# Attention and two MLPs on one core: a new planned order, input rebuilding on GpSimd, one reciprocal, late normalisation and ScalarE's Silu

## The chip, the cores and the metric

The kernel runs on one core of a Trainium2 chip. A core has five engines, each with a queue of its own that runs in the order in which the program was emitted: TensorE (PE, matmuls), VectorE (DVE), ScalarE (ACT), GpSimd (POOL) and SyncE (SP, which issues the DMAs). They meet through semaphores. The metric is device microseconds of one launch. Most executions of this kernel agree within 0.3%.

## The reference

Attention over pairwise averaged queries gives `x`, and two MLPs follow, one with a leaky rectifier, one with `h * sigmoid(h)`.

```python
# q, k, v: [2, 8, 1152, 64] float32
q_pool = q.reshape(B, H, S // 2, 2, D).mean(axis=3)          # 576 queries
scores = np.matmul(q_pool, k.transpose(0, 1, 3, 2)) / np.sqrt(D)
scores = scores - np.max(scores, axis=-1, keepdims=True)
attn = np.exp(scores)
attn = attn / (np.sum(attn, axis=-1, keepdims=True) + 1e-09)
o = np.matmul(attn, v)
x = o.transpose(0, 2, 1, 3).reshape(1152, 512)
# w_in [512, 2048], w_out [2048, 512], float64
h = x @ moe_w_in;  x = np.maximum(0.01 * h, h) @ moe_w_out
h = x @ moe2_w_in; out = (h * (1.0 / (1.0 + np.exp(-h)))) @ moe2_w_out
```

## The kernel before

**Precision.** A float32 operand is held as a high part and a low part, and a product is the sum of three matmuls (high by high, high by low, low by high). The high part is a ScalarE copy, the low part a subtraction, on GpSimd for most tiles. The weights come as float64 and are turned into float32 by bit operations: one ScalarE step (L180), four VectorE steps on an accumulator bank or a buffer (L184, L188, L192, L199), for the layer-in weights also a copy (L205) and four sums (L219), and then the split into high (L227, ScalarE) and low (L231, GpSimd).

**Attention.** `attention()` works on eight pairs of heads. Each pair has score maxima (L571), scores (L693), exponentials (L699, ScalarE), their running sums (L737, VectorE or GpSimd), the product with the values (L751), and the normalisation. `finish()` normalises the first seven pairs (L871, L874, L877: product, high part, low part). The last pair is `end()`: sums over the partitions (L837), a copy (L843), two reciprocals of 128 x 288 (L851), two products (L852), high parts (L853) and low parts (L854). The normalised values stand in `xh` and `xl`.

**MLPs.** `mlps()` works on the 1152 tokens in two groups: group 0 is 512 tokens (two halves of 256), group 1 is 640 (two halves of 320). The 2048 hidden units of a layer are four blocks. The first block of the first layer is done in the plain way (`layer_in_plain`, matmul L1283): 144 matmuls. The seven others multiply by seven products of half-size operands instead of eight (`cell`, matmul L1329), which takes sums of the inputs ahead of it and sums of the products behind it. The sums of the inputs are `transform()`: four subtractions (L1173) from the input at full precision, high parts (L1187, ScalarE) and low parts (L1193: GpSimd, but two of group 1 in the second layer on VectorE). For the first layer the full-precision input is first put together again from `xh` and `xl` by `rebuild()` (L1207, eight VectorE instructions), into `acc1`. The sums of the products are L1351 on VectorE, behind a ScalarE copy (L1365). `rectify()` makes the hidden tile `g` from a cell's result: in the first layer two ScalarE passes (L1240 the high part, L1245 the full value), in the second a sigmoid (L1255), a product on GpSimd (L1259) and a copy (L1263); then the low part (L1235, GpSimd). `layer_out_t` is the first MLP's second matmul (L1398); its result is evacuated to `acc1` (L1415 by ScalarE for the first block, L1417 by VectorE), which for the first block waits until the transform has read the rebuilt input, since both use `acc1`. `layer_out` is the second MLP's second matmul (L1464).

**Order.** Both parts are planned by a list scheduler (`Plan`): every task has an engine, a weight, a due time and the tasks that it follows; of those ready, the one due first is emitted next on its engine. So the numbers in `PARAMS` set the order of the instructions in each queue, and nothing is reordered on the chip. The MLPs run through seventeen phases: in each, two layer-in units of one block and group with the layer-out of the block and group before. Accumulators are taken in pairs of banks (`duo`), and the product sums give them back.

In what follows, `late`, `a` and `acc` are full-precision buffers, `th`/`tl` and `xh`/`xl` the high and low parts of transformed and plain inputs, `w` and `more` layer-in weights, `wout` layer-out weights, `wt` the weight in conversion, `psum` an accumulator.

## Time and profile before

| | |
|---|---|
| median of three runs | 620.33 us (619.4 to 622.56) |
| the profiled execution | 619.83 us, of which its span is 618.0 us |
| TensorE, VectorE | 591.2 us (96%), 510.3 us (83%) |
| ScalarE, GpSimd | 336.9 us (55%), 391.6 us (63%) |
| mean granted TensorE clock | 0.981 of full |

The span goes from the first to the last instruction of the core. The shares are of the whole span. The granted clock has two levels, 1.2 and 2.4 GHz; a value between them is a mean over a stretch. The attention ends, for TensorE, at 207.93 us; the first layer's steady part is from 277.02 to 376.35 us and the second layer's from 448.99 us on.

### The profile page before, as it was taken

The numbers are of one execution on the slowest core, as the hardware profiler recorded it, in microseconds if no ns is written. First come the engines' busy times: TensorE is split into PE (matmuls) and PEld (weight loads), VectorE is DVE, ScalarE is ACT, GpSimd is POOL, SyncE is SP. The second block draws the span as 40 slices with busy tenths as digits, with TensorE's granted clock in tenths as the row PEclk, the third lists the DMA queues.
The fourth block names the chain that finished last, engine by engine and source line by source line (L and its number), as shares of the span: only waits on it lengthen the run. The fifth ranks groups of instructions, "written<-read, shape, count | busy, mean of one in ns | idle before, by whom it ended". The sixth has DMA issues, their size and how long they took to land.

```text
span 618.0 us, 11491 instructions
## 1 busy us (share of the span) xinstructions
PE 591.2 (96%) x4412; PEld 506.3 (82%) x4412; DVE 510.3 (83%) x808; ACT 336.9 (55%) x573; POOL 391.6 (63%) x268
## 2 busy tenths in 40 slices
PE   7989999999999987999999999897999999999997
PEld 5758668677678676999999998886988998998986
DVE  5899779798898899758988987999887888898433
ACT  4747558567458454665545544565476644554310
POOL 7966657648450158585465464689898759759721
PEclk9799999999999988899999999999899999999999
DMA  8032433443311122232332333222132332232012
GB/s 273 35 101 55 137 98 93 149 139 94 100 33 58 53 69 69 87 118 69 102 103 74 98 101 102 66 73 68 49 94 100 100 103 90 82 103 69 0 69 85
DMA packets 33119, 55.07 MB, mean 89 GB/s; under 512 B 13196, under 2 KB 14632, under 8 KB 33064
## 3 DMA queue, kind: packets, MB, share of 16 engines
q1 hardware_dynamic: 32920, 54.14, 28.3%
q8 instruction: 34, 0.56, 0.4%
q10 hardware_dynamic: 144, 0.20, 0.1%
q14 instruction: 21, 0.17, 0.1%
HBM read 49.81 MB, written 2.42 MB: 85 GB/s over the span
## 4 chain that ended last, share of the span: by engine, by line
PE 76%; DVE 12%; ACT 5%; issue 4%; POOL 2%; DMA 1%; SPq 0%; DVEq 0%; POOLq 0%; ACTq 0%
PE psum L1329 23%; PE psum L1464 15%; PE psum L1398 14%; PE psum L693 12%; PE psum L751 7%; PE psum L564 3%; DVE acc L1173 3%; DVE late L737 2%; ACT e L699 1%; DVE mx L571 1%; DVE acc L1207 1%; PE psum L596 1%; DVE late L1351 1%; DMA qnat<-in_q_dram 1%; PE psum L789 1%
## 5 line engine op out<-in xcount | busy, mean ns | idle before, releaser
L1398 PE MATMUL psum<-g,wout 128*128 128x320 f32 (+1 forms) x576 | 106.0, 342 | 4.3 <-ACT acc L1415 3.4
L1398 PEld LDWEIGHTS psum<-g,wout 128*128 128x128 f32 x576 | 93.8, 191 | 13.3 <-ACT acc L1415 3.8
L1464 PE MATMUL psum<-wout,g 128*128 128x512 f32 (+1 forms) x444 | 100.7, 384 | 0.3 <-DVE g L1235 0.2
L699 ACT ACTIVATE e<-psum 128x512 f32<-128x512 f32 (+1 forms) x144 | 88.7, 663 | 17.4 <-PE psum L693 15.1
L571 DVE TENSOR_REDUCE mx<-psum 128x2 f32<-128x768 f32 x96 | 87.9, 949 | 10.0 <-PE psum L564 9.0
L1464 PEld LDWEIGHTS psum<-wout,g 128*128 128x128 f32 x444 | 81.1, 188 | 16.7 <-DVE g L1235 0.7
L751 PE MATMUL psum<-e,vnat 128*64 128x320 f32 (+1 forms) x576 | 72.5, 408 | 0.1
L1351 DVE TENSOR_TENSOR late<-psum,late 128x256 f32<-128x256 f32 (+3 forms) x84 | 54.5, 653 | 21.4 <-PE psum L1329 18.9
L231 POOL TENSOR_TENSOR w<-wt,w 128x896 fp32r<-128x896 f32 (+1 forms) x18 | 35.6, 1982 | 52.1 <-ACT w L227 45.7
L1235 POOL TENSOR_TENSOR g<-a,g 128x512 fp32r<-128x512 f32 (+1 forms) x34 | 48.2, 1427 | 29.4 <-ACT a L1245 26.6
L737 DVE TENSOR_TENSOR late<-late,e 128x512 f32<-128x512 f32 (+1 forms) x77 | 63.7, 862 | 0.9
L751 PEld LDWEIGHTS psum<-e,vnat 128*64 128x64 f32 x576 | 40.3, 137 | 28.3 <-ACT e L699 1.4
L737 POOL TENSOR_TENSOR late<-late,e 128x512 f32<-128x512 f32 (+1 forms) x35 | 49.9, 1425 | 21.1 <-DVE late L737 13.8
L231 POOL TENSOR_TENSOR wout<-wt,wout 128x512 fp32r<-128x512 f32 x32 | 43.5, 1374 | 22.5 <-ACT wout L227 20.8
L1329 PE MATMUL psum<-xh,w 128*128 128x256 f32 (+1 forms) x224 | 50.8, 300 | 7.3 <-DVE late L1351 7.2
L693 PE MATMUL psum<-qh,kh 64*128 64x320 f32 (+1 forms) x288 | 49.6, 341 | 1.3 <-DVE mx L571 0.5
L1329 PE MATMUL psum<-xh,more 128*128 128x256 f32 (+1 forms) x224 | 49.7, 294 | 0.6 <-DVE late L1351 0.6
L184 DVE TENSOR_SCALAR psum<-psum 128x512 f32<-128x512 f32 x60 | 41.4, 691 | 10.3 <-ACT psum L180 10.1
L231 POOL TENSOR_TENSOR more<-wt,more 128x896 fp32r<-128x896 f32 x14 | 30.2, 2162 | 23.9 <-ACT more L227 20.6
L1329 PEld LDWEIGHTS psum<-xh,w 128*128 128x128 f32 x224 | 38.3, 191 | 8.3 <-DVE late L1351 7.7
L1235 POOL TENSOR_TENSOR g<-late,g 128x512 fp32r<-128x512 f32 (+1 forms) x28 | 41.2, 1488 | 4.3 <-ACT late L1245 3.2
L693 PE MATMUL psum<-row,onesr 64*128 64x320 f32 (+1 forms) x288 | 43.1, 295 | 0.0
(123 smaller groups left out, 1422.8 us busy)
## 6 DMA issues: line engine op xcount, KB each, us to landing
wraw<-in_moe_w_in_dram SPq DMA_DIRECT2D x32, 512.0 KB, 4.0
wraw<-in_moe_w_out_dram SPq DMA_DIRECT2D x32, 512.0 KB, 3.1
vnat<-in_v_dram SPq DMA_DIRECT2D x8, 576.0 KB, 4.7
knat<-in_k_dram SPq DMA_DIRECT2D x7, 576.0 KB, 5.6
qnat<-in_q_dram SPq DMA_DIRECT2D x7, 576.0 KB, 7.4
out_dram<-acc SPq DMA_DIRECT2D x8, 256.0 KB, 2.0
xl<-late SPq DMA_DIRECT2D x7, 288.0 KB, 4.5
xh<-d SPq DMA_DIRECT2D x14, 144.0 KB, 3.9
```

Of the source, the lines that this page charges most:

```text
L184: nc.vector.tensor_scalar(out=tf, in0=tf, scalar1=2.0, scalar2=W_TOP, op0=ALU.max, op1=ALU.min)
L231: self.nc.gpsimd.tensor_tensor(out=lo, in0=tf, in1=hi, op=ALU.subtract)
L571: nc.vector.tensor_reduce(out=mx[p][:, u, c], in_=ps[:, :, 0:KC], op=ALU.max, axis=AX.X)
L693: nc.tensor.matmul(out=ps[:, j, 0:n], lhsT=lhsT[own[j], :], rhs=rhs[own[j], cs], start=m == 0, stop=m == len(terms) - 1)
L699: nc.scalar.activation(out=e_t[h, t], in_=ps[:, :, 0:n], func=ACTF.Exp, scale=scale)
L737: e.tensor_tensor(out=a, in0=e_t[h, 0] if t == 1 else a, in1=e_t[h, t], op=ALU.add)
L751: nc.tensor.matmul(out=vps[h][0][own[j], 0, 0:CW[c]], lhsT=vnat[p][:, j, t, :], rhs=e_t[h, t][:, j, :], start=(t == 0), stop=(t == NKT - 1),)
L1235: (nc.vector if fast else nc.gpsimd).tensor_tensor(out=gl, in0=a(), in1=gh, op=ALU.subtract)
L1329: nc.tensor.matmul(out=box[key][:, bank, 0:n], lhsT=w[:, i, :], rhs=y, start=(kk == 0 and q == 0), stop=(kk == 1 and q == 2),)
L1351: nc.vector.tensor_tensor(out=to, in0=p, in1=y, op=ALU.add)
L1398: nc.tensor.matmul(out=box[x][:, c, 0:n], lhsT=wt[:, ms], rhs=y[:, c * n:(c + 1) * n], start=(f == 0 and y is gh and wt is oh), stop=(f == ...
L1464: nc.tensor.matmul(out=box[x][:, c, 0:n], lhsT=y[:, ts], rhs=wt[:, cs], start=(f == 0 and y is gh and wt is oh), stop=(f == FB - 1 and y i ...
```

## The change

All of the plan's numbers are new, and several new ones are added, among them a table of the order of layer-in and layer-out in each phase (`orders`). The rest is named in the diff's pieces below.

```diff
 def end():
-            for c in range(2):
-                for j in range(2):
-                    nc.tensor.matmul(
-                        out=box["end"][own[j], c, 0:C], lhsT=ones, rhs=acc[p][:, j, c * C:(c + 1) * C], start=True, stop=True
-                    )
+            for i, j, c, rows in quarters:
+                nc.tensor.matmul(
+                    out=box["end"][rows, 0, 0:C], lhsT=ones[:, 0:32], rhs=acc[p][:, j, c * C:(c + 1) * C], start=True, stop=True
+                )
...
+        def factors():
+            nc.vector.reciprocal(out=rec[p], in_=rec[p])
+
+        def spread():
+            for i, j, c, rows in quarters:
+                nc.tensor.matmul(out=box["end"][own[j], c, 0:C], lhsT=pick[rows, :], rhs=rec[p][rows, :], start=True, stop=True)
...
 def finish(p, factors, values, due):
+        if p >= NP - 1 - P["defer"]:
...
+            later.append((
+                p % HP, norm, lambda: nc.scalar.activation(out=place(xh, p), in_=flat(), func=ACTF.Copy),
+                lambda e: e.tensor_tensor(out=place(xl, p), in0=flat(), in1=place(xh, p), op=ALU.subtract),
+            ))
+            return
...
 def mlps():
-        if ph in (2 * NBLK - 1, 2 * NBLK):
-            order += outs + ins
-        elif ph == 2 * NBLK + 1:
-            order += ins + outs
-        else:
-            order += ins[0:1] + outs + ins[1:2]
+        c = P["orders"].get(ph, (1, 0, 4))
+        order += ins[:c[0]] + outs[:c[1]] + ins[c[0]:1] + outs[c[1]:c[2]] + ins[1:] + outs[c[2]:]
...
+    def whole(layer, g):
+
+        if (layer, g) == (0, 0):
+            return late_t[:, 0:2048].rearrange("p (k n) -> p k n", k=KDM), lambda j: slice(256 * j, 256 * j + 256)
+        return acc1, lambda j: half(g, j)
...
 def transform(layer, g, after, plain_done):
-        d = P["transform"] if layer == 0 else due["in", (1, 0, g), 0] - 6.0
-        d = d + 18.0 * g * (layer == 0)
+        d = P["transform"] if layer == 0 else due["in", (1, 0, g), 0] - P["soon"]
+        d = d + P["second"] * g * (layer == 0)
...
-            fast = layer == 1 and g == 1 and m > 1
+            fast = layer == 1 and (g, m) in P["fast"]
...
 def rebuild(g, after):
-                "DVE", 0.07 + 2 * groups[g][1] / 860, P["transform"] - 1.0 + 18.0 * g,
-                lambda k=k: nc.vector.tensor_tensor(
-                    out=acc1[:, k, both(g)], in0=xh[:, k, both(g)].bitcast(F32), in1=xl[:, k, both(g)].bitcast(F32), op=ALU.add
+                "POOL", 0.13 + 2 * groups[g][1] / 435, P["rebuild"] + P["second"] * g,
+                lambda k=k: nc.gpsimd.tensor_tensor(
+                    out=held[:, k, span], in0=xh[:, k, both(g)].bitcast(F32), in1=xl[:, k, both(g)].bitcast(F32), op=ALU.add
...
 def rectify(u, f, src, a, after, d, given=(), release=None):
-        if u[0] == 0:
...
+        func = dict(func=ACTF.Silu) if u[0] else dict(func=ACTF.Prelu, alpha=0.01)
+        y = add(
+            "ACT", wa, d, lambda: nc.scalar.activation(out=three(g_slot(u, f)), in_=src(), **func), after=after,
+            take=(("g", (u, f)),),
+        )
...
 def cell(x):
-        d = due[x]
+        d = due[x] - P["cell"]
...
 def layer_out_t(x):
-        before = transformed[g] if blk == 0 else [box["acc", g, m]]
+        before = (transformed[g] if g else []) if blk == 0 else [box["acc", g, m]]
```

So the last pair's sums stand in four strips of 32 rows, one reciprocal serves them, and four matmuls with a matrix of ones in single rows (`pick`) spread the factors again. The normalisation of three more pairs is emitted by `mlps()`. The rebuilding is on GpSimd, after all pairs are normalised; group 0's goes to the attention's old buffer `late_t`. In the second MLP, Silu is applied by ScalarE to the cell's result twice (high part and full value), and GpSimd has only the low part. The product sums and the transforms are due earlier than the weight conversion on VectorE; the low parts on VectorE are now two of group 0 in the second layer. The attention's batches are three of three tiles instead of four, three and two.

Three places of the order show this. On GpSimd, in the first handover from the attention to the seven-product blocks, the queue was:

```order
L1235 TENSOR_TENSOR g_2694<-a,g_2694 128x640
L231 TENSOR_TENSOR wout_2686<-wt,wout_2686 128x512
L1193 TENSOR_TENSOR tl<-acc_2680,th 128x2x256
L231 TENSOR_TENSOR wout_2687<-wt,wout_2687 128x512
L1193 TENSOR_TENSOR tl<-acc_2680,th 128x2x256
L1193 TENSOR_TENSOR xl<-acc_2680,xh 128x2x256
L1193 TENSOR_TENSOR tl<-acc_2680,th 128x2x256
L1235 TENSOR_TENSOR g_2695<-a,g_2695 128x640
```

and it is now:

```order
L1251 TENSOR_TENSOR acc_2685<-xh,xl 128x640
L1279 TENSOR_TENSOR g_2698<-a,g_2698 128x512
L1251 TENSOR_TENSOR acc_2685<-xh,xl 128x640
L243 TENSOR_TENSOR wout_2690<-wt,wout_2690 128x512
L243 TENSOR_TENSOR wout_2691<-wt,wout_2691 128x512
L1279 TENSOR_TENSOR g_2699<-a,g_2699 128x640
L1279 TENSOR_TENSOR g_2700<-a,g_2700 128x640
L1251 TENSOR_TENSOR acc_2685<-xh,xl 128x640 x2
L243 TENSOR_TENSOR wout_2692<-wt,wout_2692 128x512
L1251 TENSOR_TENSOR late<-xh,xl 128x512 x2
L243 TENSOR_TENSOR more<-wt,more 128x896
L1251 TENSOR_TENSOR late<-xh,xl 128x512 x2
```

The rebuilds (L1251) have come in between low parts (L1279), weight splits (L243) and, behind these rows, eight transform lows (L1235) that stand ahead of the low part of `g_2695` at 640 columns.

On TensorE, at the end of the same handover, group 1's layer-out stood like this, its four tiles interleaved, with cell matmuls (L1329) ahead:

```order
L1329 MATMUL psum<-tl,more 128x256
L1329 MATMUL psum<-th,more 128x256
L1398 MATMUL psum<-g_2694,wout_2684 128x320 x6
L1398 MATMUL psum<-g_2695,wout_2685 128x320 x6
L1398 MATMUL psum<-g_2691,wout_2687 128x320 x6
L1398 MATMUL psum<-g_2690,wout_2686 128x320 x6
L1398 MATMUL psum<-g_2691,wout_2687 128x320 x6
L1398 MATMUL psum<-g_2694,wout_2684 128x320 x6
```

and it is now:

```order
L1432 MATMUL psum<-g_2699,wout_2689 128x320 x6
L1432 MATMUL psum<-g_2700,wout_2690 128x320 x6
L1432 MATMUL psum<-g_2699,wout_2689 128x320 x6
L1432 MATMUL psum<-g_2700,wout_2690 128x320 x6
L1432 MATMUL psum<-g_2699,wout_2689 128x320 x6
L1432 MATMUL psum<-g_2700,wout_2690 128x320 x6
L1432 MATMUL psum<-g_2695,wout_2691 128x320 x12
L1432 MATMUL psum<-g_2696,wout_2692 128x320 x12
L1432 MATMUL psum<-g_2695,wout_2691 128x320 x6
L1432 MATMUL psum<-g_2696,wout_2692 128x320 x6
L1432 MATMUL psum<-g_2699,wout_2689 128x320 x6
L1432 MATMUL psum<-g_2700,wout_2690 128x320 x6
```

The first two tiles (`g_2699`, `g_2700`) are multiplied for three of the four outputs first; the third (`g_2695`) comes in the seventh row here, and the cells come after all of it.

On VectorE, in the second handover, from the first MLP to the second, group 1's transform (L1173) stood among product sums (L1351), a conversion step (L184) and one of its own lows (L1193):

```order
L1351 TENSOR_TENSOR late<-psum,late 128x512
L1173 TENSOR_TENSOR acc_2680<-acc_2680 128x2x320
L1351 TENSOR_TENSOR late<-psum,late 128x512
L1173 TENSOR_TENSOR acc_2680<-acc_2680 128x2x320
L184 TENSOR_SCALAR psum<-psum 128x512
L1173 TENSOR_TENSOR acc_2680<-acc_2680 128x2x320
L1193 TENSOR_TENSOR xl<-acc_2680,xh 128x2x320
L1173 TENSOR_TENSOR acc_2680<-acc_2680 128x2x320
L1351 TENSOR_TENSOR late<-psum,late 128x256
```

and it is now:

```order
L1381 TENSOR_TENSOR late<-psum,late 128x512
L1215 TENSOR_TENSOR acc_2685<-acc_2685 128x2x320
L1381 TENSOR_TENSOR late<-psum,late 128x512
L1215 TENSOR_TENSOR acc_2685<-acc_2685 128x2x320
L1381 TENSOR_TENSOR late<-psum,late 128x512
L1215 TENSOR_TENSOR acc_2685<-acc_2685 128x2x320
L1381 TENSOR_TENSOR late<-psum,late 128x256
L1215 TENSOR_TENSOR acc_2685<-acc_2685 128x2x320
L1381 TENSOR_TENSOR late<-psum,late 128x512
```

The sums (L1381) and the subtractions (L1215) alternate, with no other step among them.

## Rows read from the trace of the kernel before

**Rows 1.** The page, engines: busy time, share, instructions of TensorE, its loads, others.

```profile
PE 591.2 (96%) x4412; PEld 506.3 (82%) x4412; DVE 510.3 (83%) x808; ACT 336.9 (55%) x573; POOL 391.6 (63%) x268
```

**Rows 2.** Table by stretch: length, busy time of each engine, clock, DMA share, GB/s.

```profile
14.00:207.93 193.93, 190.27 (x1987) 140.11 (x1987) 170.43 (x239) 119.94 (x209) 111.67 (x72) 0.98 0.31 91
207.93:277.02 69.09, 62.08 (x342) 54.95 (x341) 57.29 (x88) 38.97 (x67) 46.62 (x29) 0.93 0.27 83
277.02:376.35 99.33, 99.33 (x668) 95.52 (x667) 85.87 (x154) 51.31 (x85) 51.19 (x33) 1.00 0.29 92
376.35:448.99 72.64, 63.29 (x398) 59.65 (x397) 66.41 (x101) 41.31 (x70) 56.00 (x38) 0.95 0.24 73
418.39:423.27 4.88, 4.88 (x44) 4.88 (x43) 4.73 (x9) 1.75 (x4) 4.88 (x6) 1.00 0.33 107
448.99:614.90 165.91, 165.59 (x948) 148.16 (x947) 121.80 (x215) 79.49 (x132) 115.72 (x78) 1.00 0.25 80
```

**Rows 3.** TensorE in time, first handover: start, length, what, idle before and releaser.

```profile
214.35 1.19 PE L837 MATMUL psum<-late,ones 128*64 128x288 f32 x8
...
226.84 0.99 PE L1283 MATMUL psum<-xh,w 128*128 128x320 f32 x2 [2.96 <-ACT xh L853]
...
233.05 8.38 PE L1398 MATMUL psum<-g,wout 128*128 128x512 f32 x36
244.83 5.49 PE L1398 MATMUL psum<-g,wout 128*128 128x512 f32 x12 [3.40 <-ACT acc L1415]
...
265.32 11.71 PE L1398 MATMUL psum<-g,wout 128*128 128x320 f32 x78 [0.26 <-DVE late L1351]
```

**Rows 4.** TensorE's waits, second handover: total, times, longest.

```profile
PE psum L1329 <- DVE late L1351: 8.6, 4, 5.2
```

**Rows 5.** TensorE in time, second handover.

```profile
401.02 0.41 PE L1329 MATMUL psum<-xh,w 128*128 128x320 f32 x1 [2.00 <-DVE late L1351]
...
433.90 0.58 PE L1329 MATMUL psum<-xh,w 128*128 128x256 f32 x1 [5.20 <-DVE late L1351]
```

**Rows 6.** VectorE in time, end of the last pair's normalisation.

```profile
222.24 3.75 DVE L851 RECIPROCAL late<-late 128x288 f32<-128x288 f32 x2
...
227.19 0.81 DVE L854 TENSOR_TENSOR xl<-late,xh 128x288 fp32r<-128x288 f32 x2
```

**Rows 7.** GpSimd by shape, first handover: busy, mean ns, idle before.

```profile
L231 POOL TENSOR_TENSOR wout<-wt,wout 128x512 fp32r<-128x512 f32 x6 | 9.5, 1604 | 2.2 <-ACT wout L227 2.2
L1235 POOL TENSOR_TENSOR g<-a,g 128x640 fp32r<-128x640 f32 x4 | 6.3, 1577 | 1.2 <-ACT a L1245 1.2
L1193 POOL TENSOR_TENSOR tl<-acc,th 128x512 fp32r<-128x512 f32 x3 | 5.3, 1777 | 1.3 <-ACT th L1187 1.3
L1235 POOL TENSOR_TENSOR g<-a,g 128x512 fp32r<-128x512 f32 x4 | 5.1, 1286 | 7.8 <-ACT a L1245 7.8
L1193 POOL TENSOR_TENSOR tl<-acc,th 128x640 fp32r<-128x640 f32 x3 | 4.7, 1594 | 0.0
L231 POOL TENSOR_TENSOR more<-wt,more 128x896 fp32r<-128x896 f32 x2 | 4.3, 2127 | 7.9 <-ACT more L227 7.9
```

**Rows 8.** GpSimd in time, one instruction of each handover.

```profile
240.47 1.88 POOL L1193 TENSOR_TENSOR xl<-acc,xh 128x512 fp32r<-128x512 f32 x1
...
422.96 2.55 POOL L231 TENSOR_TENSOR wout<-wt,wout 128x512 fp32r<-128x512 f32 x2
```

**Rows 9.** VectorE in time, second handover, group 1's transform.

```profile
423.38 2.81 DVE L1173 TENSOR_TENSOR acc<-acc 128x640 f32<-128x640 f32 x1
...
426.72 0.81 DVE L1173 TENSOR_TENSOR acc<-acc 128x640 f32<-128x640 f32 x1
427.45 0.69 DVE L184 TENSOR_SCALAR psum<-psum 128x512 f32<-128x512 f32 x1
...
429.56 1.89 DVE L1193 TENSOR_TENSOR xl<-acc,xh 128x640 fp32r<-128x640 f32 x1
...
433.44 0.41 DVE L1351 TENSOR_TENSOR late<-psum,late 128x256 f32<-128x256 f32 x1
```

More of the change, by code (lines that the diff above doesn't have):

```diff
@@ L855, in steps @@
             )
-        return pe, act, (steps(0), steps(1))
+        return (pe, act, factors, spread, lambda: banks.give(box["end i"])), (steps(0), steps(1)), later
+    later = []
     def finish(p, factors, values, due):
@@ L1101, in mlps @@
     plan.rings["raw"][1].extend(("raw", n) for n in range(wt0, raw0))
+    plan.rings["wt"][1].extend(("wt", n) for n in range(P["split"], wt0))
     highs = {}
```

203 lines of the change are left out of this document (112 added, 91 removed).

## The prediction

> **What bounds the kernel now.** I read the page first: TensorE is busy for 96% of the span, VectorE for 83%, ScalarE for 55%, GpSimd for 63% [rows 1]. A change that takes no matmul away can win only where TensorE pauses or runs at its lower clock, so the second view is the table by stage [rows 2]. The reader should compare, in each stretch, its length with TensorE's busy time. From 277.02 to 376.35 us and from 448.99 to 614.90 us TensorE is busy to within 0.3 us: nothing can be won there, however much is moved on the other engines. In the attention it is 190.27 of 193.93 us. Two stretches are left, and both are handovers: 207.93 to 277.02 us (attention to the first MLP's seven-product blocks) and 376.35 to 448.99 us (first MLP to second), with 7.0 and 9.3 us without a matmul and a granted clock of 0.93 and 0.95 [rows 2].
>
> What each would last with no pause follows from TensorE's rows. A layer-out matmul takes 8.38/36 = 0.23 us at 512 columns and 11.71/78 = 0.15 us at 320 [rows 3]; the first 42 of a cell at 256 columns take 4.88 us, about 0.116 each (the 44 counted there include two cut by the edges) [rows 2]. The first stretch holds 96 matmuls of 512, 192 of 320, 42 of 256 and the end sums (1.2): 22 + 28.5 + 4.9 + 1.2 = 56.6 of 69.1 us. The second holds 48 of 512, 264 of 320 and 84 of 256: 11 + 39 + 9.8 = 59.8 of 72.6. So each loses about 13 us.
>
> The third view is TensorE in time. In the first stretch it waits 2.96 us for the last pair's normalised values and 3.40 us for a layer-out evacuation; behind the latter 12 matmuls take 5.49 us, 0.46 each, where 36 ahead of it took 0.23 each [rows 3]: the clock has fallen from its level of 2.4 GHz to 1.2 after a pause, which costs 2.7 us more. In the second it waits four times for VectorE's cell sums, 8.6 us in all [rows 4], of which 2.00 and 5.20 us are the longest [rows 5].
>
> **The change, part by part.** *One reciprocal, then a spread.* The two reciprocals run 3.75 us together, and the last low part ends 2.1 us behind them [rows 6]. Now there is one (half of 3.75), issued on sums that need half the columns, and four spreading matmuls, which I price as the end sums, 1.19 us [rows 3], at most 1.2 and at least the half. TensorE's new order is 24 matmuls, end sums, 18, spread, 54. End sums end at 215.5 as before [rows 3]; 18 by 0.23 brings 219.6, the spread 220.8, the normalised values 2.1 later 222.9. The first matmul that reads them has 6 of 512 and 18 of 320 ahead of it, 1.4 + 2.7, so it is due at 224.9. The 2.96 us wait goes, for 1.2 us of spread.
>
> *Three pairs normalised late.* Six VectorE and three ScalarE instructions leave the end of the attention for the first plain block's time. The reading matmuls are thirty and more behind; I take 0 for the path, as VectorE's 170.43 busy of 193.93 us [rows 2] leaves it slack on both sides of the boundary.
>
> *Rebuild to GpSimd, group 0's in its own tile.* Group 0's layer-out evacuation no longer waits for its transform: the 3.40 us wait and its slow 12 go. But GpSimd's queue is now in the way. The eight rebuild instructions start only once all values are normalised, 222.9. I price them by the same engine's low parts of the same shape (1.577 at 640, 1.286 at 512) [rows 7]; bounds below. Ahead of the low part of the rectified tile that the last 60 layer-out matmuls of group 1 need, the new order has 24 instructions: 4 + 4 rebuilds (6.3 + 5.1), one low at 512 and three at 640 (1.3 + 4.7), three weight splits at 1.604 (4.8), one wide split (2.1), eight transform lows (4 x 1.594 + 4 x 1.777 = 13.5) [rows 7]. The sum is 37.8, so it ends at 260.7. The third of the weight splits is 15.6 us in, at 238.5.
>
> TensorE meanwhile: 54 matmuls from 220.8 end at 229.4 (6 x 0.23 + 48 x 0.15); 18 layer-out at 0.23, 233.5; 24 at 0.15, 237.1; the next six wait for that weight split until 238.5 and end at 239.9; 24 and 24 more end at 249.0; 36 of group 1 at 254.4. Then it waits to 260.7, 6.3 us. 60 layer-out matmuls (9.0) and the cell's 42 (4.9) follow, 274.6. After a pause like this the clock was down for long enough to cost 2.7 us (above); I take 2 and get 276.6 against 277.02. **First handover: a gain of 0.4 us.** The two old waits go, and GpSimd's queue gives most of it back.
>
> The bounds: with GpSimd out of the way nothing waits, and 276.6 less 6.3, 2 and the 1.4 at the weight split is 266.9, a gain of 10.1. At the other end each instruction is held up. A 512-column low part took 1.88 us beside VectorE's own subtractions [rows 8] against 1.286 [rows 7]. With 23 at 1.88 and the wide one at 2.1 the queue takes 45.3 us, 7.5 more: a loss of 7.1.
>
> What the trace shows of such sharing: one VectorE subtraction takes 0.81 us while GpSimd is idle and 2.81 us [rows 9] while GpSimd runs two splits in 2.55 us [rows 8]. The Trainium skill, "SBUF — State Buffer", section "SBUF: two separate sides", says that the port pair which VectorE and GpSimd share is taken for a whole instruction, and that a VectorE operation with two inputs in SBUF competes for it with any GpSimd operation that reads SBUF. The trace agrees: 0.81 plus the remainder of two splits makes 2.81. By that rule the rebuild on GpSimd still competes with the transforms left on VectorE, which is the slow rival below.
>
> *Sums and transforms first on VectorE.* In the second handover the sum for which TensorE waits 5.20 us [rows 5] runs at 433.44, behind four subtractions, one conversion step of 0.69 and a transform's low part of 1.89 us [rows 9]. Now it stands behind the four subtractions alone, which alternate with sums; the low parts on VectorE are those of group 0. That brings it forward by 2.58, and leaves 2.6 us of that wait, and with it half of the slow clock behind it, whose whole I put at 2 us as in the first handover. The other three waits, 8.6 - 5.2 = 3.4 us [rows 4], fall around group 0's transform, where two conversion steps leave the same interleaving, 0.69 each; 2.0 stay. What is left is 2.0 + 2.6 + 1.0 = 5.6 of 12.8, so **7 us gained**; bounds 0 (the subtractions at 2.81 each) and 12.8 (no wait).
>
> *Silu on ScalarE.* 32 GpSimd multiplies go, at 1.3 to 1.6 us as the low parts of the same shape [rows 7], some 45 us; ScalarE keeps two passes per tile. TensorE did not wait in that stretch [rows 2], so 0. The new attention order (another batching, pauses 3.7 us in all before): 0, bounds -3 and +3.
>
> The profiled execution took 619.83 us, 1.83 beyond its span and 0.5 below the median of 620.33. 619.83 - 0.4 - 7 = **612.4**.
>
> **Rivals.** *Sums still late:* the four subtractions stay near 2.81 each, GpSimd being busy, and the second handover gives 3 instead of 7: 616.4. For it: GpSimd is busy 56.0 of 72.6 us there [rows 2]. Against: the multiplies have left it.
>
> *GpSimd's queue doesn't bind:* the normalised values come early or the lows are ready ahead, and the first handover gains its 10.1: 602.7. For it: GpSimd was busy only 46.6 of 69.1 us [rows 2]. Against: all eight rebuilds wait for the last pair, and 24 instructions stand in one row.
>
> *Slower:* GpSimd and VectorE hold each other up in both handovers, 1.88 a piece and 2.81 a subtraction: the first loses 7.1, the second gains nothing: 626.9. It makes the kernel measurably slower once the 24 instructions average about 1.73 us instead of 1.58 (3.6 us more) and the second handover is no better. For it: [rows 8, 9]. Against: in the queue's first half VectorE runs conversions, whose steps touch the accumulators.
>
> *Not felt:* the new orders let new waits in that cancel the old, attention included: 619.8.
>
> **How the numbers follow.** Forecast (606 to 615.5) 0.58, sums late 0.14, queue free 0.11, slower 0.08, not felt 0.09. The likeliest gives 612.4. The range runs from 602.5 (half of the free queue left out) to 618.5 (slower and half of the unfelt left out): some 0.18 outside. A measurement can tell about 0.5% (3.1 us) from no change, so faster means under 617.2: 0.58 + 0.11 + 0.12 of the late sums = 0.81; same 0.09 + 0.02 = 0.11; slower 0.08.
>
> **What would show it.** Right: no wait for the normalised values nor for the evacuation; one TensorE wait of 4 to 8 us near 254 for a GpSimd low part, with a lower clock behind; the second pause of 5.20 us halved; the middle and last stretches as long as before. Wrong: VectorE or ScalarE as releaser of the first handover's wait, new pauses in the attention of over 3 us, or rebuilds on GpSimd near 1.9 us.

## The result and the profile after

The changed kernel takes 611.67 us (median of four runs, 611.37 to 612.46) against 620.32 us: a ratio of 0.9857, 95% interval 0.983 to 0.9885. The profiled execution, the longest of the four, took 612.46 us; 612.4 was forecast. The total came out as said, its parts did not, and the rest of this text takes them apart.

The page, engines of the changed kernel, which answers to [rows 1]: GpSimd's busy time fell by 27 us, VectorE's by 7.

```profile
PE 589.1 (97%) x4420; PEld 506.1 (83%) x4420; DVE 503.0 (82%) x797; ACT 334.9 (55%) x573; POOL 364.6 (60%) x251
```

The table by stretch of the changed kernel, which answers to [rows 2] (columns as there). The stretches are cut where TensorE stands at the same place of the work as before: 42 cell matmuls at 320 columns have moved from behind the 48 layer-out matmuls at 512 columns to ahead of them, so the second handover begins at 379.32. Six cell matmuls at 256 columns, 0.7 us, which stood ahead of the cut before, fall behind it here.

```profile
14.00:212.15 198.15, 192.01 (x1986) 143.56 (x1987) 172.48 (x231) 120.41 (x209) 119.78 (x76) 0.97 0.32 91
212.15:280.56 68.41, 60.42 (x348) 52.27 (x347) 57.42 (x87) 38.31 (x66) 54.68 (x34) 0.98 0.24 78
280.56:379.32 98.76, 98.76 (x662) 94.87 (x661) 87.25 (x157) 52.92 (x89) 55.06 (x36) 1.00 0.30 94
379.32:441.76 62.44, 60.96 (x404) 58.37 (x403) 53.81 (x89) 40.05 (x67) 50.95 (x34) 1.00 0.22 68
441.76:607.10 165.34, 165.34 (x950) 148.31 (x948) 123.97 (x223) 78.65 (x132) 75.01 (x49) 1.00 0.26 85
```

Against before: the attention ends at 212.15 instead of 207.93 us, **4.2 us later**. The first handover takes 68.41 us where before took 68.9 (207.93 to 276.86): 0.5 gained. The second takes 62.44, or 61.7 without the six matmuls, where before took 72.6: **10.9 gained**, TensorE busy in all but 1.5 of it, its clock at full speed. The first full stretch, with the six, is as long as before (99.5 against 99.3 us), and what follows the second handover is 0.6 us shorter. Sum: -4.2 + 0.5 + 10.9 - 0.1 + 0.6 = 7.7, the span's difference.

TensorE in time, first handover of the changed kernel (answers to [rows 3]; in brackets the idle time ahead of the row and its releaser):

```profile
215.94 0.49 PE L1311 MATMUL psum<-xh,w 128*128 128x512 f32 x1 [1.39 <-ACT xh L910]
216.96 0.50 PE L1311 MATMUL psum<-xl,w 128*128 128x512 f32 x1 [0.53 <-DVE xl L913]
...
226.16 0.71 PE L865 MATMUL psum<-late,pick 32*64 32x288 f32 x8 [0.34 <-DVE late L861]
...
246.43 0.56 PE L1311 MATMUL psum<-xh,w 128*128 128x320 f32 x2 [1.92 <-ACT acc L1449]
...
253.65 3.01 PE L1432 MATMUL psum<-g,wout 128*128 128x512 f32 x12 [0.69 <-ACT acc L1449]
259.17 7.45 PE L1432 MATMUL psum<-g,wout 128*128 128x320 f32 x38 [2.50 <-ACT acc L1449]
267.07 6.14 PE L1432 MATMUL psum<-g,wout 128*128 128x320 f32 x40 [0.46 <-POOL g L1279]
```

The last pair's values hold up nothing now, and the spread (226.16) cost 0.64 us to the next matmul and a wait of 0.34. TensorE waits instead for a pair normalised inside the attention (L910, L913: 1.39 and 0.53). Evacuations no longer wait for group 0's transform, but TensorE still waits for them, three times (L1449: 1.92, 0.69, 2.50), 5.1 us where it was 3.40 [rows 3]. Last come 0.46 us for GpSimd's low part, where 6.3 was forecast. The low clock that was forecast behind that wait came behind the one of 2.50: the 38 matmuls at 259.17 take 7.45 us, 0.20 each. GpSimd's queue itself came as worked out. Its first and last rows there, of the changed kernel:

```profile
227.81 1.57 POOL L1251 TENSOR_TENSOR acc<-xh,xl 128x640 f32<-128x640 f32 x1
...
265.44 3.12 POOL L1279 TENSOR_TENSOR g<-a,g 128x640 fp32r<-128x640 f32 x2
```

From 227.81 to the end of the first of the two low parts at 267.0 are 39.2 us, 1.1 of them idle; the sum was 37.8. TensorE simply was as late as the queue: its 1.9 us ahead of the end sums and 5.1 us of evacuation waits took the place of the one long wait.

In the second handover TensorE has one wait of note left, where [rows 4, 5] had 8.6 us for sums. TensorE in time, and the eight subtractions of the transform in that stretch (length, busy time), both of the changed kernel, and then the subtractions of the kernel before:

```profile
430.39 0.41 PE L1357 MATMUL psum<-tl,more 128*128 128x320 f32 x1 [1.22 <-POOL tl L1235]
```

```profile
379.32:441.76 62.44, 6.87 (x8) 1.00 0.22 68
```

```profile
376.35:448.99 72.64, 14.28 (x8) 0.95 0.24 73
```

The eight subtractions take 0.86 us each instead of 1.79. It is not that GpSimd rests: seven of the eight still overlap one of its instructions. What changed is which starts first. VectorE and GpSimd in time, of the changed kernel:

```profile
422.39 0.81 DVE L1215 TENSOR_TENSOR acc<-acc 128x640 f32<-128x640 f32 x1
422.72 1.92 POOL L1235 TENSOR_TENSOR tl<-acc,th 128x640 fp32r<-128x640 f32 x1 [1.54 <-ACT th L1229]
423.73 1.60 DVE L1215 TENSOR_TENSOR acc<-acc 128x640 f32<-128x640 f32 x1
```

The first subtraction starts ahead of the low part and takes 0.81 us, though the low part starts within it; the second starts inside the low part and ends 0.69 us behind its end. In the kernel before, seven of the eight started inside a GpSimd instruction with 0.9 to 1.7 us of it left, and each ended 0.55 (512 columns) or 0.68 us (640) behind it, the one of 2.81 us behind the next one. Now one does; the four others that start inside one have at most a quarter of a microsecond of it left.

On these two traces the attention lost its 4.2 us at the very start. TensorE in time, first of the changed kernel and then of the kernel before (a wait, and the first product with the values), and the slow stretch as a row of the table by stretch (the number behind the five engines is the granted clock):

```profile
17.63 0.69 PE L579 MATMUL psum<-kh,qh 64*128 64x384 f32 x2 [1.84 <-ACT row L651]
...
39.13 3.24 PE L766 MATMUL psum<-e,vnat 128*64 128x256 f32 x28
```

```profile
16.47 0.58 PE L693 MATMUL psum<-qh,kh 64*128 64x256 f32 x2 [0.52 <-DVE mx L571]
...
34.46 7.87 PE L751 MATMUL psum<-e,vnat 128*64 128x256 f32 x64
```

```profile
17.57:31.20 13.63, 13.44 (x86) 11.24 (x88) 8.96 (x13) 7.60 (x18) 13.33 (x9) 0.50 0.01 1
```

```profile
15.10:21.90 6.80, 6.28 (x37) 4.48 (x35) 5.19 (x8) 4.20 (x9) 5.90 (x5) 0.50 0.24 95
```

The wait is for `row`, the first row made from the scores, and the way to it begins in SP's queue of loads. Its issues there, of the kernel before and then of the changed one:

```order
L440 DMA qnat<-in_q_dram 128x2x320
L440 DMA knat<-in_k_dram 128x1152
L440 DMA qnat<-in_q_dram 128x1152
L440 DMA vnat<-in_v_dram 128x2x576
L440 DMA knat<-in_k_dram 128x1152
```

```order
L455 DMA qnat<-in_q_dram 128x2x320
L455 DMA vnat<-in_v_dram 128x2x576 x2
L455 DMA knat<-in_k_dram 128x1152
L455 DMA qnat<-in_q_dram 128x1152
L455 DMA knat<-in_k_dram 128x1152
```

The first two loads of values now stand ahead of the second pair's keys and queries. GpSimd's first operation on those queries in time, of before and of the changed kernel, and ScalarE in time, of the changed kernel:

```profile
12.09 1.40 POOL L483 TENSOR_TENSOR qnat<-qnat 128x576 f32<-128x576 f32 x1 [0.83 <-DMA qnat<-in_q_dram]
```

```profile
15.19 1.39 POOL L498 TENSOR_TENSOR qnat<-qnat 128x576 f32<-128x576 f32 x1 [3.49 <-DMA qnat<-in_q_dram]
```

```profile
16.62 0.68 ACT L501 ACTIVATE qh<-qnat 128x576 fp32r<-128x576 f32 x1 [1.73 <-POOL qnat L498]
17.21 0.36 ACT L651 ACTIVATE row<-psum 128x256 fp32r<-128x256 f32 x1
```

The queries are there 3.1 us later (15.19 against 12.09); ScalarE's copy of them (L501) therefore waits 1.73 us, the row (L651) is queued behind the copy, TensorE waits 1.84 us for the row, and then runs at a granted clock of 0.50 for 13.6 us instead of 6.8. The first product starts 4.7 us later, and the rest of the attention keeps that distance within half a microsecond or so. Not all of this belongs to the new numbers: in no_priority (below), whose attention is the same, the clock was at 0.50 for 6.8 us alone, as before, and the attention ended at 209.3.

### The profile page after: what moved, and what is told of

It reads as the page before. It is cut to its first block, busy times and chain, and to the rows that moved or that the text cites. A ratio compares the mean times of both kernels' runs of the same rounds, so it can differ in the third digit from the quotient of the medians.

```text
span 610.3 us, 11499 instructions
## 1 busy us (share of the span) xinstructions
PE 589.1 (97%) x4420; PEld 506.1 (83%) x4420; DVE 503.0 (82%) x797; ACT 334.9 (55%) x573; POOL 364.6 (60%) x251
## 3 DMA queue, kind: packets, MB, share of 16 engines
q1 hardware_dynamic: 32920, 54.14, 28.8%
## 4 chain that ended last, share of the span: by engine, by line
PE 77%; POOL 8%; DVE 8%; issue 3%; ACT 3%; DMA 1%; SPq 0%; ACTq 0%; DVEq 0%; POOLq 0%
PE psum L1357 24%; PE psum L1498 16%; PE psum L708 12%; PE psum L1432 12%; PE psum L766 8%; DVE late L752 3%; PE psum L579 3%; POOL tl L1235 2%; PE psum L1311 1%; ACT e L714 1%; POOL late L1251 1%; PE psum L611 1%; DVE mx L586 1%; POOL xl L1235 1%; POOL xl L1467 1%
## 5 line engine op out<-in xcount | busy, mean ns | idle before, releaser
L1381 DVE TENSOR_TENSOR late<-psum,late 128x256 f32<-128x256 f32 (+3 forms) x84 | 54.6, 654 | 21.2 <-PE psum L1357 15.5
L752 POOL TENSOR_TENSOR late<-late,e 128x512 f32<-128x512 f32 (+1 forms) x37 | 52.4, 1417 | 31.5 <-DVE late L752 26.7
L752 DVE TENSOR_TENSOR late<-late,e 128x640 f32<-128x640 f32 (+1 forms) x73 | 66.1, 941 | 1.4 <-POOL late L752 0.3
L243 POOL TENSOR_TENSOR wout<-wt,wout 128x512 fp32r<-128x512 f32 x32 | 42.0, 1313 | 39.6 <-ACT wout L239 39.5
L1279 POOL TENSOR_TENSOR g<-a,g 128x512 fp32r<-128x512 f32 (+1 forms) x34 | 49.6, 1472 | 24.5 <-ACT a L1289 24.4
L243 POOL TENSOR_TENSOR w<-wt,w 128x896 fp32r<-128x896 f32 (+1 forms) x18 | 36.7, 2038 | 31.4 <-ACT w L239 29.4
L1279 POOL TENSOR_TENSOR g<-late,g 128x512 fp32r<-128x512 f32 (+1 forms) x28 | 40.0, 1437 | 18.2 <-ACT late L1289 10.5
L1357 PE MATMUL psum<-xh,w 128*128 128x256 f32 (+1 forms) x224 | 49.5, 296 | 0.2 <-ACT late L1395 0.2
L243 POOL TENSOR_TENSOR more<-wt,more 128x896 fp32r<-128x896 f32 x14 | 30.4, 2173 | 30.4 <-ACT more L239 27.9
L708 PE MATMUL psum<-qh,kl 64*128 64x320 f32 (+1 forms) x288 | 43.6, 298 | 0.0
```

The costliest lines, as they stand in the source:

```text
L243: self.nc.gpsimd.tensor_tensor(out=lo, in0=tf, in1=hi, op=ALU.subtract)
L708: nc.tensor.matmul(out=ps[:, j, 0:n], lhsT=lhsT[own[j], :], rhs=rhs[own[j], cs], start=m == 0, stop=m == len(terms) - 1)
L752: e.tensor_tensor(out=a, in0=e_t[h, 0] if t == 1 else a, in1=e_t[h, t], op=ALU.add)
L1279: (nc.vector if fast else nc.gpsimd).tensor_tensor(out=gl, in0=a(), in1=gh, op=ALU.subtract)
L1357: nc.tensor.matmul(out=box[key][:, bank, 0:n], lhsT=w[:, i, :], rhs=y, start=(kk == 0 and q == 0), stop=(kk == 1 and q == 2),)
L1381: nc.vector.tensor_tensor(out=to, in0=p, in1=y, op=ALU.add)
```

## The experiments

All medians of the changed kernels below are set against the kernel before on the same chip (620 us). The table has what each trace shows: A, the end of the attention on TensorE; from A to the first layer-out matmul of the second MLP (both handovers and the first layer); from there to the end; and the median with the ratio to before.

| kernel | A | to layer-out | to the end | median | ratio (95%) |
|---|---|---|---|---|---|
| before | 207.9 | 240.9 | 169.2 | 620.3 | |
| changed | 212.1 | 229.6 | 168.5 | 611.7 | 0.986 (0.983 to 0.989) |
| att_numbers_back | 208.8 | 226.2 | 168.5 | 605.9 | 0.977 (0.974 to 0.980) |
| att_numbers_alone | 213.2 | 244.5 | 169.2 | 627.3 | 1.009 (1.006 to 1.012) |
| silu_undone | 211.2 | 230.8 | 176.3 | 620.6 | 1.001 (0.998 to 1.004) |
| silu_alone | 209.2 | 237.7 | 171.3 | 620.5 | 1.000 (0.997 to 1.003) |
| lows_group1 | 211.9 | 232.3 | 168.4 | 614.7 | 0.992 (0.989 to 0.994) |
| no_priority | 209.3 | 232.6 | 167.0 | 611.5 | 0.986 (0.981 to 0.990) |
| phase_orders_back | 212.2 | 236.5 | 168.2 | 616.4 | 0.994 (0.991 to 0.996) |
| rebuild_on_vector | 209.7 | 236.7 | 168.9 | 616.6 | 0.994 (0.991 to 0.996) |
| ab_two_reciprocals | 211.2 | 231.7 | 168.6 | 613.1 | 0.987 (0.983 to 0.992) |
| ab_no_late_pairs | 209.3 | 227.0 | 168.6 | 608.1 | 0.981 (0.977 to 0.985) |
| ab_shared_acc | 209.2 | 241.2 | 170.9 | 623.0 | 1.005 (1.003 to 1.006) |
| ab_subtraction_weight | 210.4 | 224.0 | 172.1 | 607.7 | 0.981 (0.974 to 0.988) |

(In no_priority six layer-out matmuls, 1.4 us, come ahead of the cut; the cut is at the other 54.) The medians rest on 4 to 10 executions each, and those of one kernel differ by 1.1 to 7.8 us; the kernel before took 617.3 to 624.8 us over 29 executions. A differs too where the attention is the same: it lies between 209.3 and 212.3 us in the six traces of the changed kernel and its variants with the new numbers, and between 208.8 and 211.2 in att_numbers_back and the three variants of it that keep its pairs. So where an edit leaves the attention alone, its effect is read behind A.

The theory to be tested first: the second handover was won by VectorE's order, the first was a draw, and the attention's loss comes from its start. The rivals: GpSimd's relief won the second, and the attention's later end is the price of the first.

### The attention's numbers

**att_numbers_back.**

```diff
-    load1=10.25, prep=(-0.08, -21.22, 15.55, 10.41), batches=((0, 1, 2), (3, 4, 5), (6, 7, 8)),
+    load1=0.47, prep=(-2.45, -18.91, 13.33, 10.72), batches=((0, 1, 2, 3), (4, 5, 6), (7, 8)),
...
```

> The changed kernel with the attention's numbers (batches, due times, last_three, last_pool) as they were; everything of the MLPs as changed. Theory: the changed kernel's attention ends 4.2 us later (212.15 against 207.93 us) only because TensorE waits 1.84 us at 17.63 us for a ScalarE row and then runs at its low clock until 31 us; with the old numbers that wait is gone, the attention ends near 208 us, the two handovers stay as they are (68.4 us to the first full stretch, 161.2 us from there to the second layer's layer-out), and the time is 607.5 us. Rival: the longer attention had made room for the MLPs' first weights and normalisations; then the first handover grows by what the attention wins, and the time stays within 610.5 to 612.5 us.

605.94 us (605.43 to 607.14), 5.7 below the changed kernel, more than the theory said; the rival, by which the time stays, falls. TensorE in time:

```profile
16.47 0.58 PE L708 MATMUL psum<-qh,kh 64*128 64x256 f32 x2 [0.76 <-DVE mx L586]
...
34.76 7.61 PE L766 MATMUL psum<-e,vnat 128*64 128x256 f32 x62
```

The wait for the row is gone, and the first product starts at 34.76 us, as before. Beyond that the way to the layer-out is 3.4 us shorter (226.2 instead of 229.6), all of it in the first handover: the waits for L910 and L913 are gone too, and the clock stays at full speed there (1.00 against 0.98). The new numbers leave VectorE later with its sums: the last one ends 3.8 us behind A in the changed kernel and 0.1 ahead of it here. The second handover is as long as in the changed kernel.

**att_numbers_alone.** The opposite: the kernel before with the new numbers.

```diff
-    load1=0.47, prep=(-2.45, -18.91, 13.33, 10.72), batches=((0, 1, 2, 3), (4, 5, 6), (7, 8)),
+    load1=10.25, prep=(-0.08, -21.22, 15.55, 10.41), batches=((0, 1, 2), (3, 4, 5), (6, 7, 8)),
...
```

> The kernel before with the attention's new numbers alone. Theory: they bring the ScalarE row at 17.6 us and the low clock until 31 us, and with it 4 to 6 us more: 624 to 626 us. Rival: the start is slow in the changed kernel for another reason (the ones matrix for the spread, set up on GpSimd ahead of it): 619 to 621 us.

627.30 us (624.23 to 628.90). The wait for the row is 1.93 us at 17.63, the first product starts at 39.07 us, and the way to the layer-out is 3.6 us longer. The kernel before has no `pick`, so the rival, by which setting up that matrix delays the start, falls. Both directions agree: these numbers cost 6 to 7 us; on the traces 3.3 and 5.3 of it lie ahead of A and some 3.5 behind. In att_numbers_back SP's queue has the order of before again; that order was not put back by itself, so the way from the loads to the wait is read from the trace, not shown by a run.

### The second handover

**phase_orders_back.**

```diff
-    orders={1: (1, 0, 2), 2: (0, 4, 4), 4: (0, 4, 5), 5: (0, 2, 3), 6: (1, 0, 4), 7: (1, 0, 4), 8: (0, 4, 5), 9: (1, 0, 0), 10: (1, 0, 4), 11: (1, 0, 3), 16: (1, 0, 2)},
...
+    orders={0: (1, 0, 9), 1: (1, 0, 9), 2: (1, 0, 9), 3: (1, 0, 9), 4: (1, 0, 9), 5: (1, 0, 9), 6: (1, 0, 9), 7: (0, 9, 9), 8: (0, 9, 9), 9: (1, 0, 0), 10: (1, 0, 9), 11: (1, 0, 9), 12: (1, 0, 9), 13: (1, 0, 9), 14: (1, 0, 9), 15: (1, 0, 9), 16: (1, 0, 9), 17: (1, 0, 9)},
...
```

> The changed kernel with the order of layer-in and layer-out in each phase as before (the table `orders` replaced by the old rule, group 0's layer-out ahead of the cells in the phases around the second handover). Theory: TensorE's new order there (the cells of the first layer's last block between the layer-outs) gives VectorE and GpSimd the time for the transforms and won most of the 10.8 us; then 5 to 9 us are lost: 617 to 620 us. Rival: the handover was won by the low parts moved to group 0 and by the multiplies gone from GpSimd, which stay: 611 to 613 us.

616.43 us (614.51 to 618.80): 4.8 lost, just under what the theory said. Its trace, of the longest of ten executions, is 6.7 us longer. The 48 matmuls at 512 columns begin at 382.64 and the layer-out at 448.8: 66.2 us. In the changed kernel it is 55.6 (386.19 to 441.76) with 48 cell matmuls, 6.9 us, ahead; so 3.7 us are lost here, and the rest in the first handover, whose phases are in the table too: there TensorE waits 4.55 us at 270.74 for the low part that cost it 0.46. Of the second handover's gain, the order of the phases is the largest single part found.

**lows_group1.**

```diff
-    fast=((0, 1), (0, 3)),
+    fast=((1, 2), (1, 3)),
```

> The changed kernel with the two transform low parts on VectorE taken from group 1 of the second layer, as before, instead of group 0. Theory: they stand among the sums that TensorE waits for, 1.6 to 1.9 us each, and some 2.5 us of the second handover's gain is lost: 614 us, with a wait of 2 to 4 us for a VectorE sum near 428 us. Rival: what freed the sums was the removal of the weight conversion from among them, and the low parts are hidden: 611 to 612.5 us; below nothing too, since GpSimd's low part was what TensorE waited for there (1.22 us): 610.5 us.

614.69 us (614.07 to 616.38), 3.0 lost; from the 512-column block to the layer-out 58.5 us (385.78 to 444.24) instead of 55.6. But TensorE's waits there are 1.72 us for GpSimd's low part (1.22 in the changed kernel) and 0.94 for ScalarE, not for a sum, and its clock falls for one more stretch (0.97 of full from 379.0 to 444.3). The size is the theory's; the wait named was not.

**no_priority.**

```diff
-    soon=318.9, cell=51.0,
+    soon=6.0, cell=0.0,
```

> The changed kernel with the due times of product sums and of the second layer's transforms as they were (no lead of 51 us for sums, 6 instead of 318.9 us for transforms), so that the weight conversion stands among them again. Theory: this order won the second handover, and 5 to 10 of its 10.8 us are lost: 617 to 622 us, with waits for VectorE sums between 400 and 440 us. Rival: the handover was won by the new order of the phases on TensorE and by GpSimd's relief, and VectorE has room for both: 611.5 to 613 us.

611.47 us (609.26 to 612.91): nothing lost that a measurement can tell. On this trace the way to the layer-out is longer by 1.6 us (3.0, less the six layer-out matmuls' 1.4). The theory falls: sums and transforms ahead of the conversion, on which the prediction put the whole 7 us, are worth 1.6 us on this trace, given the other parts. What they would be worth alone, in the kernel before, was not tried; with the other parts in place they are not needed.

**silu_undone** and **silu_alone**: the activation back in the changed kernel, and alone in the kernel before.

```diff
-        func = dict(func=ACTF.Silu) if u[0] else dict(func=ACTF.Prelu, alpha=0.01)
...
+            y = add("ACT", wa, d, sigmoid, after=after, take=("t",))
...
+                "POOL", wp, d, lambda: nc.gpsimd.tensor_tensor(out=a(), in0=a(), in1=box["t", u, f], op=ALU.mult),
...
+                "ACT", wa, d, lambda: nc.scalar.activation(out=g_slot(u, f), in_=a(), func=ACTF.Copy),
...
```

> The changed kernel with the second MLP's activation as it was: sigmoid on ScalarE, product on GpSimd, copy on ScalarE; 32 GpSimd multiplies more, some 45 us of GpSimd. Theory: the second handover was won by VectorE's order, and TensorE is full behind it, so the multiplies cost nothing: 611 to 612.5 us. Rival: the gain came from GpSimd having less to do when the transform's low parts are due; then the low parts of group 1 come 2 to 5 us later and the time is 614 to 617 us.

> The kernel before with one part of the change alone: Silu by ScalarE instead of sigmoid, GpSimd product and copy. Theory: TensorE never waited for the multiplies, so the second layer's steady part (169.2 us behind 448.82) stays, and the second handover wins at most the 1 to 2 us by which GpSimd's multiplies held up subtractions and low parts around 429 us: 618 to 620.5 us. Rival: the multiplies are what the second handover waited for by way of the shared ports; then it wins 5 us or more: under 616 us.

silu_undone takes 620.55 us (618.41 to 624.46): 8.9 lost, and neither side had the place. The second handover has one wait of note, 1.24 us where the changed kernel has 1.22; the loss is behind it, 176.3 us to the end instead of 168.5. TensorE there waits for hidden tiles, and its clock falls behind the first wait (7 matmuls in 3.35 us):

```profile
462.50 3.35 PE L1516 MATMUL psum<-wout,g 128*128 128x512 f32 x7 [2.31 <-POOL g L1280]
...
563.07 6.65 PE L1516 MATMUL psum<-wout,g 128*128 128x512 f32 x28 [1.40 <-POOL g L1280]
```

silu_alone takes 620.50 us (617.59 to 624.07), no change, as the theory said (its trace has a way to the layer-out shorter by 3.2 and an end longer by 2.1 us). The rival, that GpSimd's relief won the second handover, falls twice: with the multiplies back the eight subtractions take 7.4 us in all, and in the old order without them 14.8. So the multiplies were free in the old order and are not in the new one, in which the layer-outs come earlier and `rectify()` later (26.1 us behind the due time instead of 5): in this change Silu keeps the rest of the gain, and is no gain by itself. That the later due time is what uncovers the multiplies is argued from the order; sigmoid and multiply with the old due time were not tried.

### The first handover

**rebuild_on_vector.**

```diff
-                "POOL", 0.13 + 2 * groups[g][1] / 435, P["rebuild"] + P["second"] * g,
-                lambda k=k: nc.gpsimd.tensor_tensor(
+                "DVE", 0.07 + 2 * groups[g][1] / 860, P["transform"] - 1.0 + P["second"] * g,
+                lambda k=k: nc.vector.tensor_tensor(
```

> The changed kernel with the eight rebuilds on VectorE, as due as the transforms, and group 0's still in its own tile. Theory: VectorE is busy for 9 to 10 of 10 us in most of the first handover, and 8 rebuilds of 0.7 to 1.9 us more (6 to 12 us) push the weight conversion and the transforms back; the evacuations, which wait in ScalarE's queue behind steps of the conversion, come later, and the handover grows from 68.4 us by 2 to 6 us: 614 to 618 us. Rival: GpSimd's queue of 24 instructions is what bounds the handover (it ended at 267.0 us, 0.46 us after TensorE wanted it); with 11.5 us less in it TensorE gains up to 3 us: 608.5 to 611 us.

616.61 us (615.78 to 620.09), 4.9 lost; on the trace 7.1 on the way to the layer-out, with an attention that ended 2.4 us earlier. TensorE in time:

```profile
242.18 1.22 PE L1432 MATMUL psum<-g,wout 128*128 128x512 f32 x2 [3.21 <-ACT wout L239]
244.93 3.03 PE L1432 MATMUL psum<-g,wout 128*128 128x512 f32 x6 [1.53 <-POOL wout L243]
250.32 4.63 PE L1432 MATMUL psum<-g,wout 128*128 128x512 f32 x10 [2.36 <-POOL wout L243]
```

The waits are for the layer-out weights, whose conversion VectorE now does later, and the clock is low in all three rows (2 matmuls in 1.22 us in the first; it stood at 0.50 from 242.2 to 255.8). So GpSimd, slower as it is, was the right place: its queue ended when TensorE came.

The four that follow are built on att_numbers_back (605.9 us).

**ab_two_reciprocals.** The end of the last pair as before: sums in full width, two reciprocals, no spread.

```diff
-            nc.vector.reciprocal(out=rec[p], in_=rec[p])
...
+                lambda: nc.vector.reciprocal(out=r(), in_=r()),
...
```

> The changed kernel with the attention's old numbers (605.9 us), and the last pair's end as before: sums spread at once over 128 rows, two reciprocals of 128 x 288, no spreading matmuls. Theory: the single reciprocal is what took the 2.96 us wait for the last pair's values away; the wait comes back by 2 to 3 us, less the 0.6 us of the spread, and GpSimd's rebuilds start as much later: 607.5 to 609 us. Rival: the handover is bound by the evacuations in ScalarE's queue, which are due at the same time either way, and the wait is only moved: 605.5 to 606.5 us.

613.11 us (608.93 to 613.58), 7.2 lost, more than either side said. But on its trace 2.4 us of it lie ahead of A, in an attention whose instructions are the same, and are not the reciprocal's. VectorE in time, four running sums of att_numbers_back and the same four here:

```profile
87.58 3.53 DVE L752 TENSOR_TENSOR late<-late,e 128x640 f32<-128x640 f32 x4
```

```profile
88.28 6.88 DVE L752 TENSOR_TENSOR late<-late,e 128x640 f32<-128x640 f32 x4
```

One of them takes 3.05 us instead of 0.82: here GpSimd came first with a subtraction of 3.19 us, and TensorE waits 2.48 us for the sum. What the edit costs is the 5.5 us behind A (231.7 against 226.2). No wait for the last pair's values comes back. There are waits for weights (1.42, 1.85) and for an evacuation:

```profile
256.14 5.49 PE L1428 MATMUL psum<-g,wout 128*128 128x512 f32 x12 [3.92 <-ACT acc L1445]
```

12 matmuls take 5.49 us behind it, at the low clock, as in [rows 3]. All waits of the first handover together are 7.9 us against 6.9 in att_numbers_back, and the clock is 0.93 instead of 1.00, so most of the 5.5 is the clock behind the waits. That VectorE's longer way is what moved the waits is argued.

**ab_no_late_pairs.**

```diff
-    defer=3,
+    defer=0,
```

> The changed kernel with the attention's old numbers, and all seven pairs normalised in the attention (none late). Theory: nine instructions move back over a boundary on both sides of which VectorE has slack with the old numbers: 605 to 607 us. Rival: they keep VectorE, 11.69 of 13.00 us busy at the attention's end, from the last sums, and TensorE waits: 608 to 610 us.

608.12 us (606.36 to 610.12): the median is the rival's, two of the four executions are the theory's. Its trace is 1.2 us longer (604.8 against 603.6), with waits of 1.07, 1.87 and 0.83 us early in the handover and shorter ones for evacuations. By median and trace the late pairs bring some 1 to 2 us.

**ab_shared_acc.** Group 0's inputs in the shared buffer, the evacuation waiting again.

```diff
-        if (layer, g) == (0, 0):
+        if False:
...
-        before = (transformed[g] if g else []) if blk == 0 else [box["acc", g, m]]
+        before = transformed[g] if blk == 0 else [box["acc", g, m]]
```

> The changed kernel with the attention's old numbers, and group 0's inputs rebuilt into the buffer of the layer-out's results as before, so that the evacuations wait for its transform again. Theory: group 0's transform is done some 10 us after its first evacuation is due, two accumulator pairs stay taken, and TensorE waits 8 us or more, its clock falling: 614 to 620 us. Rival: TensorE finds other work in the meantime, as it waited only 3.4 us in the kernel before: 608 to 610 us.

623.02 us (621.76 to 624.24), 17.1 lost, more than the theory's 8 to 14. One row has it:

```profile
258.94 0.90 PE L1311 MATMUL psum<-xh,w 128*128 128x320 f32 x2 [18.39 <-ACT acc L1449]
```

With the rebuild on GpSimd, the own tile is not worth the 3.4 us of before but 17: without it the kernel is slower than the kernel before (ratio 1.005).

**ab_subtraction_weight.**

```diff
-        w = 0.2 + 2 * n / 600
+        w = 0.2 + 2 * n / (430 if layer == 0 else 600)
```

> The changed kernel with the attention's old numbers, and the planner's weight of a first-layer transform subtraction raised to what the trace shows beside GpSimd (1.7 us at 640 columns instead of 1.27), which puts two evacuations ahead of a weight split in ScalarE's queue. Theory: the first handover's waits of 1.93 and 2.50 us for evacuations, each behind such a split, shrink to under 1 us each, and the time is 602 to 604 us. Rival: the evacuations come ahead and the split late, and GpSimd's low part (1.07 us of wait now) binds instead: 605 to 607 us.

607.65 us (604.99 to 612.82). The handover did what the theory said: its waits of over 0.5 us fell to three of 0.7 to 0.8, and the way to the layer-out is 224.0 us, the shortest of all. The time was not the theory's 602 to 604: every later order changed with it, behind the layer-out a cell waits for a weight split, the clock falls there, and the end takes 172.1 instead of 168.5 us.

```profile
466.63 0.41 PE L1357 MATMUL psum<-xh,w 128*128 128x256 f32 x1 [2.04 <-POOL w L243]
```

So a gain of 2.2 us was more than given back in the last stretch (another 1.6 us lie in the attention, which the edit leaves alone); att_numbers_back stays the fastest kernel found, by its median.

## Why the prediction was right, and where it was not

**Right:** the places and the total. Both full stretches stayed full, and what moved by more than 1 us lies in the handovers and the attention. That the total came out to 0.1 us is luck: the attention lost 4.2 us that were not forecast, and the second handover gained 3.9 more than forecast. By its own signs the prediction did not hold in the first handover either: an evacuation does hold up TensorE, ScalarE is the releaser of its four longest waits, no wait of 4 to 8 us for a low part came, and three of the four rebuilds at 512 columns took about 1.85 us.

**The first handover, 0.4 forecast and 0.5 measured,** is right in sum and in GpSimd's queue (37.8 against 39.2 us), wrong in what TensorE waits for. The step that failed is "TensorE meanwhile": it let ScalarE evacuate at once and took the earlier pairs as normalised. In ScalarE's queue two evacuations stand behind a split of the next layer-in weights, which waits for VectorE, and these two are 4.4 of the 5.1 us; with the evacuations ahead (ab_subtraction_weight) each wait is 0.7. The slow rival's condition (24 instructions at 1.73 us) was not met: 1.63 each, idle time included. Its mechanism is in the trace all the same: rebuilds at 512 columns took up to 1.87 us where 1.29 was the price.

**The spread** was priced at 1.19 us and took 0.64. **One reciprocal** was worth a wait of 2.96 in the sum and 5.5 us behind A in the experiment, where the low clock counts more than the waits. **The late pairs**, taken as 0, are worth 1 to 2 us. **The own tile**, taken as 3.4 and its slow matmuls, is worth 17 with the rebuild where it now is.

**The second handover, 7 forecast and 10.9 measured,** is the term that was mis-sized, and its step that failed is the cause: "sums and transforms first on VectorE". Undone, that costs 1.6 us on the trace and nothing that the medians tell. Of the parts that were undone one at a time, the order of phases on TensorE holds 3.7 us and the low parts moved to group 0, which the prediction did count, 3. The rival "sums still late" fell: three of group 1's four subtractions take 0.8 to 0.9 us and one 1.60, none 2.81. All eight take 6.9 us instead of 14.3 (9.6 with the old phases, 8.7 without the priority), because all but one now start ahead of a GpSimd instruction or in its last quarter of a microsecond; what that alone is worth to TensorE was not tried. What is left of the 10.9 has not been told apart.

**The attention, 0 forecast with bounds of 3,** lost 4.2 on the profiled execution and was outside its bounds. The step took the pauses of the old attention as the measure of what a new order may cost; it left out SP's queue, past which the new numbers move two loads of values, and what the clock makes of one early wait. The other traces with the same attention end it 1.3 to 4.3 us later than before, the later the longer the low clock lasted.

**Silu, 0 forecast,** is right for Silu alone, and wrong as a part of this change: 8.9 us hang on it. "TensorE did not wait in that stretch" was true of the old order only.

Two sums of the prediction are a little low by its own prices: 192 matmuls at 0.15 us are 28.8, not 28.5, and 48, 264 and 84 at 0.23, 0.15 and 0.116 are 60.5, not 59.8. The second handover, with nothing but 1.5 us of pauses left in it, has 61.0 us of matmuls, the six of above among them.

## What to carry to other kernels

A large change of a plan is a sum of gains and losses by stage: undo the numbers of one stage at a time, for here one stage's numbers cost 6 us that another's had won, and the kernel without them is the fastest found (605.9 us). Undoing a part shows what it is worth while the others stand, and no more. Read such an edit behind the place where it can first act: ahead of it, traces of the same instructions differed by up to 2.4 us. A step that costs nothing because other work covers it is covered only in that order: after a reorder the multiplies cost 8.9 us and the shared buffer 17.1, as much as the whole gain and more. Moving work to a slower engine paid here, where the faster one stands ahead of everybody's inputs.

## What the runs showed of the hardware

One early wait of 1.84 us was followed by 13.6 us at a granted clock of 0.50 in the changed kernel, where 6.8 us stood before. The length is not the same in each trace: no_priority, whose attention is the changed kernel's, waited 2.00 us at 17.33, was at 0.50 from 16.6 to 23.4 us and at full speed from there on, and its first product started at 36.27 us instead of 39.13. The other traces with the new numbers lie between 36.7 and 39.3; those with the old lie between 34.5 and 34.8, but for two (silu_alone, ab_no_late_pairs) at 36.3. So the old numbers alone leave a spread of 1.8 us, the new ones one of 3.0, and where a single trace falls in it is not explained by these runs. Where the low clock lasted 6.8 us with either, the new ones start the first product at 36.3 and 36.7 us, the old at 34.5 to 34.8: some 2 us are the numbers' own.

A subtraction of 128 x 640 on VectorE took 0.81 us when GpSimd was idle at its start and 2.81 when it started with 2.13 us left of GpSimd's splits [rows 8, 9]; at 426.72 in [rows 9] GpSimd's next instruction came 0.3 us into the subtraction and did not lengthen it. GpSimd's rebuild of 128 x 512 took 1.28 to 1.87 us. The Trainium skill, "SBUF — State Buffer", section "SBUF: two separate sides", has the shared ports held for a whole instruction. The trace agrees for VectorE: over both kernels' second handovers a subtraction that starts inside a GpSimd instruction ends 0.5 to 0.7 us behind it (once behind the next), and one that starts first is not lengthened. The fall from 14.28 to 6.87 us for eight is what it is worth to start first. The Trainium skill, "GPSIMD Engine Reference", in its introduction, calls GpSimd the wrong choice for elementwise arithmetic, VectorE being about twice as fast. The instructions agree (1.58 against 0.81 us at 640 columns), the kernel does not: with the rebuild on VectorE it is 4.9 us slower.
